# The order of the score groups within a head pair, in a windowed-attention and gated-MLP kernel

## The chip, the cores and the metric

The kernel runs on one core of a Trainium2 chip. The metric is the device time of one execution in microseconds (us); lower is better. A core has five engines with instruction streams of their own: PE (TensorE, matrix multiplications and transposes), ACT (ScalarE, exponentials, GELU and copies), DVE (VectorE, elementwise work), POOL (GpSimd) and SP (SyncE, which issues DMAs). Each engine takes its instructions in program order; between engines, semaphores hold an instruction back until what it needs is there.

## The reference, cut to what matters

Attention with a window of 128 positions and 4 sink positions, over a batch of 4, 8 heads, 768 positions and 64 values a head; then a gated MLP block over the 512 attention outputs of a position.

```python
scores = scale * np.matmul(q, k.transpose(0, 1, 3, 2))
keep = is_sink | in_window          # pos < 4, or 0 <= rel < 128
a = np.exp(np.where(keep, scores, -1e9) - max); a = a / a.sum(-1)
x = np.matmul(a, v)                 # heads side by side: 768 x 512 per batch
h = gelu(x @ w_in); u, v = halves of h
v_n = (v - mean) / sqrt(var + 1e-6) * g_ln
v_s = einsum('ts,bsd->btd', w_sg, v_n) + b_sg
out = x + (u * v_s) @ w_out
```

## The kernel before, in words

The work is cut into 16 head pairs, n = 0 to 15, four to a batch. The order of all instructions is written out by hand: the program order of the Python text is the order on each engine, and nothing reorders it. PSUM has these pools: `ps_s`, two buffers for scores; `ps_t`, one buffer for the transposes of k and q; `ps_a`, one for the attention outputs; `ps_m`, two for the MLP's products.

For each pair the main loop does the following.

- `repack` (L182): POOL casts k and q of pair n + 2 to bf16, and issues the load of v.
- `score(n, g)` (L223, L227), for g = 0, 1, 2: four matmuls on PE, two for each head, put the scores of 256 keys into one `ps_s` buffer. The two heads lie on rows 0 to 63 and 64 to 127, so these matmuls use 64 rows each (64*128 in the profile), where all others use 128. One exponential on ACT takes the scores from PSUM to the tile `ex`.
- `values(n - 1, i)` (L268, L271, L274), for i = 0 to 5: the pair before is multiplied with its v; i = 0 to 2 go behind score 0 and i = 3 to 5 behind score 1. After each three, DVE divides by the sums (L278, L279).
- `keys(n + 1)` (L188, L195): behind score 0's values, PE transposes k of the next pair into `ps_t`, and ACT copies that to `kT`. POOL copies the sink keys (L205) from it to a tile `sk`.
- `keep_band(n, g)` (L234): DVE multiplies the exponentials by the mask.
- `queries(n + 1)` (L188, L195): behind score 1's values and mask, PE transposes q of the next pair, and ACT copies that to `qT`. From pair 4 on this goes through `ps_t`, the buffer that the keys use; before, through `ps_m`.
- `spread`: puts in fillers, which are pieces of the batch before: `spatial_weights` (L171), then eight spatial groups (L346 on PE, L349 and L352 on DVE) and six projections (L357 on PE, L360 on DVE).
- `sinks(n)` (L238, L240): one matmul of 128 rows gives the scores of the sink positions for the later queries, in a `ps_s` buffer, and one exponential on ACT takes them to `exs`. It stands behind the fillers of g = 2.

After each pair whose number can be divided by 4 (from pair 4 on), the remaining fillers are put out and the hidden stage of the finished batch follows (`hidden`: L296, L298, L300 for one half of h, L308, L311 for the other), with the values of that pair in between. The pair behind it (5, 9, 13) therefore has no values of a pair before it, and its first exponential comes behind an ACT table load, since the hidden stage uses GELU. Pair 15 has no next pair, hence no `keys` and no `queries`.

Of the kernel before, what the change touches and what calls it, by code (L numbers as in the profile page):

```python
# [17 lines left out]
def kernel(  # L18
# [23 lines left out]
    HP = H // 2  # L42
# [31 lines left out]
    def load_qk(n):  # L74
        b, hp = divmod(n, HP)
        pair = []
        for src, name in ((k, "k_sb"), (q, "q_sb")):
            dst = loads.tile([128, 2, NT, 64], F32, name=name)
            nc.sync.dma_start(out=dst, in_=src[b, 2 * hp:2 * hp + 2].rearrange(
                "h (p t) d -> p h t d", t=NT))  # L80
            pair.append(dst)
        qk[n] = pair

    def load_v(n):
        b, hp = divmod(n, HP)
        nc.gpsimd.dma_start(  # L86
            out=v_bufs[n % NV][:, :, :, 0:64],
            in_=v[b, 2 * hp:2 * hp + 2].rearrange("h (t p) d -> p h t d", p=128))
# [61 lines left out]
    def load_weights(n):  # L150
        if n < 4:
            half = slice(DF, d_ff) if n < 2 else slice(0, DF)
            cs = slice(KD // 2 * (n % 2), KD // 2 * (n % 2 + 1))
            nc.gpsimd.dma_start(
                out=w_in_sb[:, cs, half],
                in_=moe_w_in.rearrange("(c p) f -> p c f", p=128)[:, cs, half])
        elif n == 4:
            for c in (slice(0, HT), slice(HT, NT)):
                nc.gpsimd.dma_start(
                    out=wsg_sb[:, c, :],  # L160
                    in_=moe_w_sg.rearrange("(c p) s -> p c s", p=128)[:, c, :])
        elif n == 5:
            nc.gpsimd.dma_start(out=b_bc, in_=moe_b_sg.partition_broadcast(128))
            nc.gpsimd.dma_start(out=g_sb, in_=moe_g_ln.rearrange("(c p) -> p c", p=128))
            nc.gpsimd.dma_start(out=w_out_sb,
                                in_=moe_w_out.rearrange("(c p) f -> p c f", p=128))
# [11 lines left out]
    def repack(n, eng):  # L178
        packed[n] = []
        for src, name in zip(qk.pop(n), ("k_bf", "q_bf")):  # L180
            flat = work.tile([128, NT, 128], BF16, name=name)
            eng.tensor_copy(flat.rearrange("p t (h d) -> p h t d", h=2), src)  # L182
            packed[n].append(flat)
# [15 lines left out]
    def keys(n):  # L199
        kT, sk = kT_bufs[n % NB], sk_bufs[n % NB]  # L200
        kps = to_columns(packed[n][0], ps_t, "tp")
        copy(nc.scalar, kT, kps)
        for hl in range(2):
            rows = slice(64 * hl, 64 * hl + 64)
            nc.gpsimd.tensor_copy(sk[rows, 32 * hl:32 * hl + n_sink], kT[rows, 0:n_sink])  # L205

    def queries(n, eng, pool, tag):
        qps = to_columns(packed.pop(n)[1], pool, tag)
        qTs[n] = work.tile([128, S], BF16, name="qT")
        copy(eng, qTs[n], qps)  # L210

    def score(n, g):
        kT, qT = kT_bufs[n % NB], qTs[n]
        if g == 0:
            exps[n] = work.tile([128, NT * 512 - 256], BF16, name="ex")
        ex = exps[n]
        sc = ps_s.tile([128, 2, 512], F32, name="sc", tag="s")
        w = 0
        for j in (2 * g, 2 * g + 1):
            n_q = min(256, S - 128 * j)  # L220
            for hl in range(2):
                rows = slice(64 * hl, 64 * hl + 64)
                nc.tensor.matmul(sc[:, hl, w:w + n_q], kT[rows, 128 * j:128 * (j + 1)],  # L223
                                 qT[rows, 128 * j:128 * j + n_q], start=True, stop=True)
            w += n_q
        part = ex[:, 1024 * g:1024 * g + 2 * w].rearrange("p (h c) -> p h c", h=2)
        nc.scalar.activation(out=part, in_=sc[:, :, 0:w], func=AF.Exp, scale=scale)  # L227

    def keep_band(n, g):
        w = 1024 if g < HT - 1 else 768  # L230
        part = exps[n][:, 1024 * g:1024 * g + w]
        m = mask0 if g == 0 else mask
        m = m.rearrange("p a c -> p (a c)") if g < HT - 1 else mask_end
        nc.vector.tensor_mul(part, part, m)  # L234

    def sinks(n):
        scs = ps_s.tile([128, 2, 512], F32, name="scs", tag="s")
        nc.tensor.matmul(scs[:, 0, 0:NS], sk_bufs[n % NB], qTs.pop(n)[:, 256:S],  # L238
                         start=True, stop=True)
        nc.scalar.activation(out=exs_bufs[n % NB][0:32 + n_sink],  # L240
                             in_=scs[0:32 + n_sink, 0, 0:NS], func=AF.Exp, scale=scale)

    def by_dma(n):
        return n >= HP and n % HP < HP - 1

    def columns(n):
        b, hp = divmod(n, HP)
        xps = to_columns(x_sb[b][:, hp], ps_m, "mm")
        nc.vector.tensor_copy(xT[b][:, hp, :], xps.rearrange("c t p -> c (t p)"))  # L249

    def values(n, i):
        b, hp = divmod(n, HP)
        if hp == 0 and i == 0:
            x_sb[b] = work.tile([128, HP, NT, 128], BF16, name="x")
            xT[b] = work.tile([128, HP, S], BF16, name="xT")
        ex, exs, v_sb = exps[n], exs_bufs[n % NB], v_bufs[n % NV]
        c, m = divmod(i, HT)
        if m == 0:
            avs[n] = ps_a.tile([128, HT, 2, 65], F32, name="av", tag="av")
        av = avs[n]  # L260

        def probs(j, hl, half):
            at = 1024 * (j // 2) + hl * min(512, S - 256 * (j // 2) + 128)
            at += 256 * (j % 2) + 128 * half
            return ex[:, at:at + 128]

        for hl in range(2):
            nc.tensor.matmul(av[:, m, hl, :], probs(i, hl, 0), v_sb[:, hl, i, :],  # L268
                             start=(m == 0 and hl == 0), stop=False)
            if i >= 1:  # L270
                nc.tensor.matmul(av[:, m, hl, :], probs(i - 1, hl, 1),  # L271
                                 v_sb[:, hl, i - 1, :], start=False, stop=False)
        if i >= 2:
            nc.tensor.matmul(av[:, m], exs[:, 128 * (i - 2):128 * (i - 1)],  # L274
                             vsink[:, n], start=False, stop=(m == HT - 1))
        if m == HT - 1:
            rcp = inverses[:, 2 * n + c]
            nc.vector.reciprocal(rcp, av[:, :, :, 64:65])  # L278
            nc.vector.tensor_mul(  # L279
                x_sb[b][:, hp, HT * c:HT * (c + 1), :].rearrange(  # L280
                    "p i (h d) -> p i h d", h=2),
                av[:, :, :, 0:64], rcp.to_broadcast([128, HT, 2, 64]))
        if i == NT - 1 and by_dma(n):
            nc.sync.dma_start_transpose(
                out=xT[b][:, hp, :].rearrange("p (i q) -> p i q", i=NT),
                in_=x_sb[b][:, hp].rearrange("p i d -> p (i d)"))
# [80 lines left out]
    def fill(count=1):  # L367
        for _ in range(count):
            if fillers:
                fillers.pop(0)()  # L370
# [147 lines left out]
    for n in range(NP):  # L518
        if n + 2 < NP:
            repack(n + 2, G)  # L520
            load_v(n + 2)
        load_weights(n)
        value = (lambda i: values(n - 1, i)) if n > 0 and valued < n - 1 else (lambda i: None)
        points = (HT + 1) * ((HP - n) % HP)

        def spread(left):
            fill(-(-len(fillers) // (points + left)))

        for g in range(HT):
            score(n, g)  # L530
            if g < 2:
                for i in range(HT * g, HT * (g + 1)):
                    value(i)
            if g == 0 and n + 1 < NP:
                keys(n + 1)
                if n < HP:
                    queries(n + 1, A, ps_m, "mm")
            keep_band(n, g)
            if g == 1 and n + 1 < NP and n >= HP:
                queries(n + 1, A, ps_t, "tp")  # L540
            spread(HT + 1 - g)
        if n + 3 < NP:
            load_qk(n + 3)
        sinks(n)
        if n > 0 and valued < n - 1 and not by_dma(n - 1):
            columns(n - 1)
        spread(1)
        valued = n - 1
        if n % HP == 0 and n > 0:
            fill(len(fillers))  # L550
            hidden(n // HP - 1, [lambda i=i: values(n, i) for i in range(NT)])
            valued = n
# [51 lines left out]
```

## Time and profile before

| | |
|---|---|
| median of 3 runs | 185.49 us (185.37 to 187.05) |
| profiled execution | 184.96 us, its span 183.1 us |
| PE busy | 156.4 us, 85% of the span |
| DVE busy | 150.6 us, 82% |
| ACT busy | 115.7 us, 63% |
| POOL busy | 58.3 us, 32% |
| pair 5 begins | 43.88 us after the span's start |
| pair 15's score 0 | 139.88 us |

The span runs from the first to the last instruction; the rest of the execution's time lies around it. A row of the profile names an engine, a line of the kernel, an operation, and what it writes and reads ("ex<-sc"). Behind a bar come the busy time in total, the mean duration of one in ns, and the idle time of the engine just before these instructions with what ended it. In a timeline a row gives the start, the duration, the engine and the line; a bracket at its end holds the idle time before it and what released it. PE's matmuls overlap each other: one of 384 columns lasts 0.33 us, and the next starts 0.16 us after it.

### The profile page before, as it was taken

What the parts mean: (1) busy time and instruction counts of PE and PEld (TensorE: products, weight loads), DVE (VectorE), ACT (ScalarE), POOL (GpSimd) and SP (SyncE); (2) the same over time, 40 slices, a digit from 0 to 9 for tenths busy, and PEclk for the clock granted to TensorE, in tenths of its full rate; (3) what the DMA queues carried; (4) which work ended last, traced back from release to release, by engine and by line L of the source; (5) the groups of instructions that cost most, each with busy time, mean ns of one, the idle gap of its engine ahead of it and who ended that gap; (6) DMA issues with size and microseconds to landing.
All of it is one profiled execution on the core that took longest, in us unless ns stands there. A gap on an engine that the chain in (4) does not pass through costs nothing.

```text
span 183.1 us, 3710 instructions
## 1 busy us (share of the span) xinstructions
PE 156.4 (85%) x1397; PEld 88.4 (48%) x1407; DVE 150.6 (82%) x362; ACT 115.7 (63%) x159; POOL 58.3 (32%) x98
## 2 busy tenths in 40 slices
PE   0679778799689999899799998998999979998950
PEld 0436555456456555455455544563564444544410
DVE  5676888699779998698899988699999977888850
ACT  2398999767828668666967778778875706630000
POOL 7569999930050161422051070650000000000000
PEclk9999999999789999999999999999999999999997
DMA  5999999999934769996248579976202551000081
GB/s 178 251 313 251 259 271 270 187 203 227 189 58 32 215 68 257 307 186 46 56 162 82 173 223 186 363 57 42 47 0 43 132 194 67 0 0 4 27 294 39
DMA packets 47289, 27.27 MB, mean 149 GB/s; under 512 B 33632, under 2 KB 44128, under 8 KB 47264
## 3 DMA queue, kind: packets, MB, share of 16 engines
q1 hardware_dynamic: 19360, 20.65, 37.7%
q0 software_dynamic: 27904, 6.31, 36.6%
q8 instruction: 13, 0.21, 0.5%
q14 instruction: 12, 0.10, 0.2%
HBM read 24.81 MB, written 6.29 MB: 170 GB/s over the span
## 4 chain that ended last, share of the span: by engine, by line
PE 58%; DVE 17%; ACT 13%; issue 4%; DMA 3%; SPq 1%; POOL 1%; DVEq 0%
PE vs L346 13%; PE o_ps L357 11%; ACT ex L227 6%; PE sc L223 6%; PE hv L296 6%; PE hu L308 6%; PE cps L188 5%; DVE st L300 4%; PE av L268 4%; DMA q_sb<-in_q_dram 3%; ACT kT L195 2%; DVE vn L336 2%; PE av L271 2%; PE wps L171 2%; PE av L274 2%
## 5 line engine op out<-in xcount | busy, mean ns | idle before, releaser
L227 ACT ACTIVATE ex<-sc 128x1024 bf16<-128x1024 f32 (+1 forms) x48 | 45.6, 958 | 17.6 <-PE sc L223 17.3
L346 PE MATMUL vs<-wsgT,vn 128*128 128x384 bf16 x192 | 36.4, 326 | 3.3 <-DVE vn L336 1.4
L346 PEld LDWEIGHTS <-vn 128*128 128x128 bf16 x192 | 17.8, 98 | 16.6 <-DVE vn L336 4.0
L234 DVE TENSOR_TENSOR ex<-ex,mask 128x1024 bf16<-128x1024 bf16 x32 | 22.7, 709 | 3.6 <-ACT ex L227 3.6
L296 PE MATMUL hv<-w_in_sb,xT 128*128 128x512 bf16 x93 | 22.7, 379 | 2.2 <-DVE xT L249 1.7
L182 POOL CAST k_bf<-k_sb 128x768 bf16<-128x768 f32 x15 | 12.7, 847 | 36.9 <-DMA k_sb<-in_k_dram 22.4
L357 PE MATMUL o_ps<-w_out_sb,gT 128*128 128x512 bf16 x89 | 23.4, 379 | 0.9 <-DVE o_sb L360 0.6
L308 PE MATMUL hu<-xT,w_in_sb 128*128 128x384 bf16 x128 | 23.6, 325 | 0.0
L298 ACT ACTIVATE v_all<-hv 128x512 f32<-128x512 f32 x24 | 14.3, 597 | 11.8 <-PE hv L296 11.5
L349 DVE SCALAR_TENSOR_TENSOR gv<-vs,g_sb,b_bc 128x384 bf16<-128x384 f32 x32 | 19.6, 613 | 1.2 <-PE vs L346 1.2
L300 DVE BATCH_NORM_STATS2 st<-v_all 128x6 f32<-128x512 f32 x24 | 16.4, 682 | 4.9 <-ACT v_all L298 4.8
L223 PE MATMUL sc<-qT,kT 64*128 64x256 bf16 x192 | 19.1, 282 | 1.3 <-DVE qT L197 1.0
L268 PE MATMUL av<-v_sb,ex 128*128 128x65 bf16 x192 | 19.0, 198 | 1.4 <-DVE x L279 1.4
L311 ACT ACTIVATE uT<-hu 128x384 bf16<-128x384 f32 x32 | 15.7, 490 | 7.1 <-PE hu L308 6.9
L268 PEld LDWEIGHTS <-ex 128*128 128x128 bf16 x192 | 14.8, 100 | 9.0 <-issue 2.5
L279 DVE TENSOR_TENSOR x<-av,inverses 128x384 bf16<-128x384 f32 x32 | 17.8, 557 | 1.1
L360 DVE TENSOR_TENSOR o_sb<-o_ps,x 128x512 f32<-128x512 f32 x24 | 16.5, 688 | 2.0 <-PE o_ps L357 1.7
L205 POOL COPY sk<-kT 64x4 bf16<-64x4 bf16 x32 | 6.6, 206 | 34.4 <-ACT kT L195 33.5
L271 PE MATMUL av<-v_sb,ex 128*128 128x65 bf16 x160 | 17.3, 197 | 0.0
L86 POOL DMA_DIRECT2D v_sb<-in_v_dram x16 | 16.6, 1036 | 0.0
L182 POOL CAST q_bf<-q_sb 128x768 bf16<-128x768 f32 x15 | 14.6, 972 | 5.0 <-PE hu L308 2.1
L308 PEld LDWEIGHTS <-w_in_sb 128*128 128x128 bf16 x128 | 12.1, 97 | 8.3 <-issue 1.2
(72 smaller groups left out, 231.3 us busy)
## 6 DMA issues: line engine op xcount, KB each, us to landing
k_sb<-in_k_dram SPq DMA_DIRECT2D x16, 384.0 KB, 5.4
q_sb<-in_q_dram SPq DMA_DIRECT2D x16, 384.0 KB, 6.2
out_dram<-o_sb SPq DMA_DIRECT2D x24, 256.0 KB, 3.5
v_sb<-in_v_dram POOLq DMA_DIRECT2D x16, 192.0 KB, 7.2
wsg_sb<-in_moe_w_sg_dram POOLq DMA_DIRECT2D x2, 576.0 KB, 9.9
w_in_sb<-in_moe_w_in_dram POOLq DMA_DIRECT2D x4, 256.0 KB, 9.2
w_out_sb<-in_moe_w_out_dram POOLq DMA_DIRECT2D x1, 512.0 KB, 11.2
b_bc<-in_moe_b_sg_dram POOLq DMA_DIRECT2D x1, 384.0 KB, 10.0
```

Source lines behind the costliest of these rows:

```text
L182: eng.tensor_copy(flat.rearrange("p t (h d) -> p h t d", h=2), src)
L223: nc.tensor.matmul(sc[:, hl, w:w + n_q], kT[rows, 128 * j:128 * (j + 1)], qT[rows, 128 * j:128 * j + n_q], start=True, stop=True)
L227: nc.scalar.activation(out=part, in_=sc[:, :, 0:w], func=AF.Exp, scale=scale)
L234: nc.vector.tensor_mul(part, part, m)
L268: nc.tensor.matmul(av[:, m, hl, :], probs(i, hl, 0), v_sb[:, hl, i, :], start=(m == 0 and hl == 0), stop=False)
L271: nc.tensor.matmul(av[:, m, hl, :], probs(i - 1, hl, 1), v_sb[:, hl, i - 1, :], start=False, stop=False)
L296: nc.tensor.matmul(h_ps, xT[b][:, c, 128 * j:128 * (j + 1)], w_in_sb[:, c, DF:], start=(c == 0), stop=(c == KD - 1))
L300: nc.vector.bn_stats(out=st, in_=v_alls[b][:, j, :])
L308: nc.tensor.matmul(h_ps[:, 0:NH], w_in_sb[:, c, 128 * f:128 * (f + 1)], xT[b][:, c, NH * n:NH * (n + 1)], start=(c == 0), stop=(c == KD - 1))
L346: nc.tensor.matmul(vs[:, 0:NH], vns[b][:, si, 128 * f:128 * (f + 1)], wsgT[:, si, cols], start=(si == 0), stop=(si == NT - 1))
L349: nc.vector.scalar_tensor_tensor(out=gv, in0=vs[:, 0:NH], scalar=g_sb[:, f:f + 1], in1=b_bc[:, cols], op0=ALU.mult, op1=ALU.add)
L357: nc.tensor.matmul(o_ps, gTs[b][:, c, 128 * t:128 * (t + 1)], w_out_sb[:, c, :], start=(c == 0), stop=(c == KU - 1))
```

## The change

From pair 5 on (`n > HP`, with HP = 4), `score(n, 0)` and `score(n, 1)` are both put out at g = 0, with their exponentials, ahead of the values, the keys' transposes and the fillers of that step. At g = 1 no score is put out; the values 3 to 5, the mask, the queries and the fillers keep their places. At g = 2 `score(n, 2)` is followed at once by `sinks(n)`, which before stood behind the mask, the fillers of that step and the issue of the next loads. Pairs 0 to 4 stay as they are, and so do all shapes, tiles and buffers.

```diff
+        def pending(g):
+            if n > HP:
+                if g == 0:
+                    score(n, 0)
+                    score(n, 1)
+                elif g == 2:
+                    score(n, 2)
+                    sinks(n)
+            else:
+                score(n, g)
+
         for g in range(HT):
-            score(n, g)
+            pending(g)
             if g < 2:
                 for i in range(HT * g, HT * (g + 1)):
                     value(i)
@@
             spread(HT + 1 - g)
         if n + 3 < NP:
             load_qk(n + 3)
-        sinks(n)
+        if n <= HP:
+            sinks(n)
         if n > 0 and valued < n - 1 and not by_dma(n - 1):
             columns(n - 1)
         spread(1)
```

## The prediction

> **What bounds the kernel now.** I read the page first, then the time by stage, then the engines' own timelines pair by pair from pair 5 on (pairs count from 0), since only pairs 5 to 15 change. From the page:
>
> ```profile
> PE 156.4 (85%) x1397; PEld 88.4 (48%) x1407; DVE 150.6 (82%) x362; ACT 115.7 (63%) x159; POOL 58.3 (32%) x98
> ...
> L195 ACT COPY kT<-cps 128x768 bf16<-128x768 bf16 x16 | 12.7, 794 | 4.0 <-PE cps L188 4.0
> ```
>
> PE and DVE are both near full, ACT is not; an average says no more. The view by stage says more (columns: stretch, its length, busy time of PE, PEld, DVE, ACT, POOL, granted clock, DMA):
>
> ```profile
> 44.66:48.07 3.41, 1.55 (x24) 1.14 (x22) 2.54 (x6) 3.40 (x4) 0.37 (x2) 1.00 1.10 119
> 48.07:51.49 3.42, 3.42 (x29) 2.69 (x29) 2.70 (x5) 1.86 (x3) 0.82 (x1) 0.50 0.83 250
> 126.58:129.99 3.41, 2.22 (x18) 1.13 (x17) 3.08 (x7) 3.40 (x5) 0.36 (x2) 1.00 0.29 58
> 94.58:101.51 6.93, 6.93 (x77) 4.12 (x77) 6.67 (x16) 4.88 (x6) 2.21 (x4) 1.00 0.61 59
> ```
>
> The last row is pair 10: PE is busy for all of its 6.93 us, DVE for 6.67. In this pair PE is the bound and nothing that it issues waits; a wait added to PE there is paid in full as soon as DVE's small slack is no obstacle. The first three rows come back below, for the clock. Now pair 10 on PE and on ACT:
>
> ```profile
> 94.58 0.39 PE L223 MATMUL sc<-qT,kT 64*128 64x256 bf16 x4
> ...
> 95.28 0.50 PE L188 MATMUL cps<-iden,k_bf 128*128 128x128 bf16 x6
> 95.62 1.14 PE L346 MATMUL vs<-wsgT,vn 128*128 128x384 bf16 x6
> 96.69 0.39 PE L223 MATMUL sc<-qT,kT 64*128 64x256 bf16 x4
> 97.01 0.20 PE L268 MATMUL av<-v_sb,ex 128*128 128x65 bf16 x1
> ...
> 97.56 0.50 PE L188 MATMUL cps<-iden,q_bf 128*128 128x128 bf16 x6
> ```
>
> ```profile
> 95.02 1.02 ACT L227 ACTIVATE ex<-sc 128x1024 bf16<-128x1024 f32 x1 [0.71 <-PE sc L223]
> 95.94 0.79 ACT L195 COPY kT<-cps 128x768 bf16<-128x768 bf16 x1
> 97.12 1.02 ACT L227 ACTIVATE ex<-sc 128x1024 bf16<-128x1024 f32 x1 [0.39 <-PE sc L223]
> 98.09 0.80 ACT L195 COPY qT<-cps 128x768 bf16<-128x768 bf16 x1
> ```
>
> The reader should see the order on ACT: first exponential, copy of kT, second exponential, copy of qT. The transposes of k and of q share the single buffer of ps_t, so PE's q transposes (97.56) can't start before ACT has emptied it into kT (95.94 + 0.79 = 96.73). Here that leaves 0.83 us of slack. Where the slack is gone, in the first pair after a batch's hidden stage, it is a wait already:
>
> ```profile
> 127.25 1.02 ACT L227 ACTIVATE ex<-sc 128x1024 bf16<-128x1024 f32 x1
> 128.17 0.79 ACT L195 COPY kT<-cps 128x768 bf16<-128x768 bf16 x1
> ...
> 129.01 0.49 PE L188 MATMUL cps<-iden,q_bf 128*128 128x128 bf16 x6 [0.28 <-ACT kT L195]
> ```
>
> ```profile
> 45.31 0.39 PE L223 MATMUL sc<-qT,kT 64*128 64x256 bf16 x4
> 47.55 0.49 PE L188 MATMUL cps<-iden,q_bf 128*128 128x128 bf16 x6 [1.85 <-ACT kT L195]
> ```
>
> **The change, part by part.** No instruction is added or removed; three moves are made.
>
> *Move 1, on PE: score 1 directly behind score 0.* Score groups use 64 rows, all else 128 (the 64*128 and 128*128 in the rows). In pair 10 six L346 start 0.1625 us apart from 95.62, so the next slot is 96.595; after them comes score 1, and the values start at 97.01. The group with both changes of row form costs 0.42 us. The two score groups that already stand together in pair 0 start 0.40 us apart at 0.19 us between matmul starts, against 0.12 here, which makes about 0.23 us at this speed. So each merged group gives back 0.19 us of PE, 2.1 us over 11 pairs if nothing else moved; bounds 0.15 to 0.22. The Trainium skill, "TensorEngine Tiling (Array Packing)", Key Properties, says that changing the tiling mode drains TensorE; that speaks for the change, and it gives no price, so the sum stays with the rows.
>
> *Move 2, on ACT: the second exponential goes ahead of the kT copy.* This follows from the same edit, since each score issues its exponential. ACT then runs exponential, exponential, kT copy. From exponential to the next instruction ACT takes 0.92 us (95.02 to 95.94); for an exponential behind an exponential, pair 0 has one place (two merged, the second a short one of 0.81):
>
> ```profile
> 10.95 1.73 ACT L227 ACTIVATE ex<-sc 128x1024 bf16<-128x1024 f32 x2
> ```
>
> 1.73 - 0.81 is 0.92 again. So the kT copy starts 0.92 us later, measured from the first exponential. With T the start of score 0, the first exponential starts at T + 0.44, the kT copy at T + 2.28, ends at T + 3.07, and the q transposes can go at T + 3.12 (0.05 from copy end to PE, as at 128.17 + 0.79 and 129.01). PE arrives there at T + 2.98 - 0.19 = T + 2.79 in pairs whose filler is a spatial group (6, 7, 10, 14), and at T + 2.68 where it is a shorter projection (8, 11, 12: 2.87 in the trace, from 68.01 to 70.88). So PE now waits 0.33 and 0.44 us where it waited for nothing. Net of the 0.19 gained: +0.15 us in each of four pairs and +0.25 in each of three. Behind the waiting transposes on PE stand the next filler, score 2, the sink scores and two fillers; DVE's product or projection sum, ACT's qT copy and the third exponential wait for those, so the next thing late is everything. The bounds: -0.19 if the wait were covered, +0.35 if the exponentials slip by another 0.1.
>
> In pairs 5, 9 and 13 an ACT table load stands ahead of the first exponential (it starts at T + 1.9) and PE already waits for kT. There PE's 0.19 only lengthens the wait, and the whole 0.92 us is paid: q transposes at 129.93 instead of 129.01. Bounds 0.85 (a little regained from idle PE) and 1.3 (pair 5, where part of the following work falls to the half clock below).
>
> Pair 15 has no next pair, hence no kT copy: PE gains 0.19, but DVE works there without a gap from 139.99 to 145.90, and its first reciprocal would now wait 0.08 us for values that start later; I take -0.1, bounds -0.2 to 0.
>
> *Move 3: the sink scores directly behind score 2, ahead of a filler.* They join no row form (128*128), so no change is saved. Cost taken: 0. The cover: their exponentials are first read in the next pair's values, over 3 us later, their PSUM buffer (score 1's) was emptied over 2 us before, and the filler that they push back by 0.22 us feeds a DVE that is still on the last mask (100.19 to 100.75, with the filler's product at 100.66). If that cover were gone it would cost up to 0.2 us in each of 11 pairs; bounds 0 to +1 us in all. Queues: POOL's two small copies behind kT move by 0.92 us and POOL idles for microseconds around them; no wait moves past SP's loads, whose buffers the casts free as before.
>
> *Sum on the path:* 3 x 0.92 + 4 x 0.15 + 3 x 0.25 - 0.1 = **+4.0 us**.
>
> **The clock.** The first stage row shows a stretch of 3.41 us with PE busy 1.55 us; the next 3.42 us ran at a granted clock of 0.50. The third row shows 2.22 us busy, and the rows after it stay at 1.00. So somewhere between 1.55 and 2.22 us of work the clock is lost, for one stretch. After the change, PE in pair 13 has only two lone L346 (0.33 each) between 126.83 and 129.93; a stretch laid over that has about 1.0 us of work, well under 1.55, while one whose edge falls in the middle has over 2. Pair 9 is alike. Where the edges fall I can't know from one execution: with about half of all positions hitting, one of the two pairs is likeliest. Half a clock for 3.41 us costs 1.7 us of PE work, less some 0.2 spent waiting anyway: **+1.5 us**; bounds 0 and 3.0 for none and both. The Trainium skill, "TensorE: Matmul & The Clock Gate", What's actually happening, says that the clock halves after at least one idle window of some 3.4 us. Read strictly, 1.7 us of unbroken idle would not do it and the time would be that of the rival without a half stage; but the 44.66 row had a break of 1.85 us only and lost the clock, so I go by the row.
>
> 184.96 us, the profiled execution's own time (span 183.1 and 1.9 around it), + 4.0 + 1.5 = 190.5. The median of the runs, 185.49, lies 0.5 above that execution, so **191.0**.
>
> **The rivals.**
> *No further half stage* (0.26): waits as computed, the edges fall kindly or the threshold is lower: 189.5. For it: 2.22 us of work was enough.
> *Two half stages* (0.18): pairs 9 and 13 both, 192.5. Against it: a loss in pair 9 shifts pair 13 by about half a stretch.
> *DVE takes up the waits* (0.07): if DVE, not PE, set the pace (6.67 of 6.93 us), the 0.15 and 0.25 us would vanish in its backlog and only 3 x 0.92 remain: 185.49 + 2.7 = 188.2. Against it: in pair 10 no PE instruction waits for DVE.
> *The saved form changes win* (0.06), not slower: if PE reached the q transposes after the kT copy, all 11 merged groups would keep 0.19 us: 185.49 - 2.1 = 183.4. It decides if the copy ends before T + 2.7, that is 0.4 us sooner than I compute, or if the second exponential stood behind the copy on ACT. Against it: the program order of ACT. Half of it caught would be no change.
>
> **How the numbers follow.** The forecast has 0.43. The range 188.6 to 193.0 reaches from the rival with DVE's backlog to both half stages, with the bounds on the sink move. Within 1% is about what a measurement of this kernel can tell from no change; faster by over 1% gets 0.04, within 1% 0.05, slower 0.91.
>
> **What would show it.** Right: on ACT two exponentials in a row from pair 5 on, then kT; the q transposes waiting for kT in ten pairs, with 0.15 to 0.3 us of idle PE in seven (the profile counts from a matmul's end, some 0.16 us after the next could have started) and over 1.4 us in three; PE's idle before kT in total some 7 us instead of 2.6; a second stretch at 0.50 clock. Wrong: no wait before the q transposes, DVE with no gaps, or score groups that don't start about 0.23 us apart.

## The result, and the profile after

The changed kernel is slower: 191.38 us, the median of 4 runs (190.5 to 193.08), against 185.61 us for the kernel before on the same chip. The ratio is 1.034, with a 95% interval of 1.029 to 1.040. The forecast was 191.0 us, in a range of 188.6 to 193.0. Here and below, a ratio leaves out runs that lie more than 1.5% above the fastest of their kernel, so it can differ a little from the ratio of the medians.

The profiled execution is the slowest of the four, 193.08 us with a span of 191.3. Some 2.3 us of its distance to the profile before lies ahead of the change: pair 5 begins at 46.18 us instead of 43.88, because POOL waits longer for the first loads of k and q. So the pairs are compared by their lengths.

The page again, with its row of the q transposes, and then what PE waited for there, before and after:

```profile
PE 155.7 (81%) x1392; PEld 90.5 (47%) x1407; DVE 149.9 (78%) x362; ACT 114.5 (60%) x159; POOL 60.0 (31%) x98
...
L188 PE MATMUL cps<-iden,q_bf 128*128 128x128 bf16 x96 | 9.5, 245 | 10.4 <-ACT kT L195 8.5
```

```profile
PE cps L188 <- ACT kT L195: 2.6, 3, 1.8
```

```profile
PE cps L188 <- ACT kT L195: 8.5, 10, 2.9
```

The busy times hardly changed, and the span did. PE's idle time ahead of the q transposes that ends with the copy to kT is 8.5 us, in ten waits of at most 2.9; before it was 2.6 us, in three. This line names the place of the cost. Its size needs the stages too, since PE also saves some 2 us and loses clock.

The stages: pairs 6, 9 and 13 before.

```profile
54.39:61.31 6.92, 6.92 (x77) 4.11 (x77) 6.66 (x16) 4.88 (x6) 0.43 (x2) 1.00 0.65 62
...
86.97:94.58 7.61, 6.42 (x50) 3.27 (x49) 6.92 (x16) 6.51 (x8) 1.20 (x3) 1.00 0.48 131
...
125.34:132.96 7.62, 6.43 (x51) 3.29 (x51) 7.08 (x16) 6.51 (x8) 0.36 (x2) 1.00 0.14 28
```

And after. First the stretch that ends where the second half-clock stretch begins, that stretch, and one that kept its clock; then whole pairs: 6, 9 and 13.

```profile
91.84:95.25 3.41, 1.39 (x8) 0.41 (x6) 2.71 (x6) 3.40 (x4) 0.00 (x0) 1.00 0.39 71
95.25:98.66 3.41, 3.15 (x16) 1.59 (x17) 1.24 (x3) 0.96 (x3) 1.97 (x4) 0.50 0.66 217
132.80:136.21 3.41, 1.79 (x14) 0.82 (x13) 2.50 (x6) 3.38 (x5) 0.00 (x0) 1.00 0.29 58
...
57.38:64.44 7.06, 6.71 (x76) 4.31 (x77) 6.76 (x16) 4.71 (x6) 0.54 (x2) 1.00 0.62 61
...
90.86:100.85 9.99, 7.57 (x50) 3.83 (x51) 6.89 (x15) 6.49 (x8) 3.41 (x5) 0.83 0.37 100
...
132.23:140.76 8.53, 6.14 (x49) 3.28 (x49) 6.49 (x15) 6.49 (x8) 0.81 (x2) 1.00 0.12 25
```

An ordinary pair takes 7.06 us instead of 6.92, and PE is no longer busy all through it. Pair 13 takes 8.53 instead of 7.62. Pair 9, in which the clock halves, takes 9.99 instead of 7.61. Pair 10 on ACT and PE:

```profile
101.28 1.94 ACT L227 ACTIVATE ex<-sc 128x1024 bf16<-128x1024 f32 x2 [1.36 <-PE sc L223]
103.11 0.81 ACT L195 COPY kT<-cps 128x768 bf16<-128x768 bf16 x1
104.49 0.80 ACT L195 COPY qT<-cps 128x768 bf16<-128x768 bf16 x1 [0.58 <-PE cps L188]
```

```profile
100.85 0.61 PE L223 MATMUL sc<-qT,kT 64*128 64x256 bf16 x8
101.77 0.50 PE L188 MATMUL cps<-iden,k_bf 128*128 128x128 bf16 x6
102.10 1.14 PE L346 MATMUL vs<-wsgT,vn 128*128 128x384 bf16 x6
103.96 0.49 PE L188 MATMUL cps<-iden,q_bf 128*128 128x128 bf16 x6 [0.18 <-ACT kT L195]
```

The two exponentials stand in a row (x2), the copy ends at 103.92, and the q transposes start at 103.96, 3.11 us after score 0. And pair 9:

```profile
92.76 1.94 ACT L227 ACTIVATE ex<-sc 128x1024 bf16<-128x1024 f32 x2
94.59 0.81 ACT L195 COPY kT<-cps 128x768 bf16<-128x768 bf16 x1
```

```profile
92.75 0.79 PE L346 MATMUL vs<-wsgT,vn 128*128 128x384 bf16 x2 [0.20 <-DVE vn L336]
95.44 0.80 PE L188 MATMUL cps<-iden,q_bf 128*128 128x128 bf16 x6 [1.90 <-ACT kT L195]
96.04 2.12 PE L346 MATMUL vs<-wsgT,vn 128*128 128x384 bf16 x6
```

PE stands idle for 1.90 us, and then six L346 take 2.12 us instead of 1.14: the work behind the wait runs at half speed. The lengths of the pairs, in us, before, after, and by forecast:

| pairs | before | after | difference | forecast |
|---|---|---|---|---|
| 5 | 10.51 | 11.20 | +0.69 | +0.92 |
| 6, 7, 10, 14, each | 6.92 (7: 6.70) | 7.06 (7: 6.84) | +0.14 | +0.15 |
| 8, with the hidden stage | 18.96 | 19.58 | +0.62 | +0.25 |
| 11; 12 with the hidden stage | 6.48; 17.35 | 6.73; 17.60 | +0.25 each | +0.25 each |
| 9 | 7.61 | 9.99 | +2.38 | +0.92, and 1.5 for the clock |
| 13 | 7.62 | 8.53 | +0.91 | +0.92 |

From pair 5 to pair 14 that is 5.6 us in all, and by forecast 4.1 for the order on ACT and 1.5 for the clock.

### The profile page after: what moved, and what is told of

Same layout as the page of the kernel before. It is cut to its first block, busy times and chain, and to the rows that moved or that the text cites. A ratio compares the mean times of both kernels' runs of the same rounds, so it can differ in the third digit from the quotient of the medians.

```text
span 191.3 us, 3715 instructions
## 1 busy us (share of the span) xinstructions
PE 155.7 (81%) x1392; PEld 90.5 (47%) x1407; DVE 149.9 (78%) x362; ACT 114.5 (60%) x159; POOL 60.0 (31%) x98
## 4 chain that ended last, share of the span: by engine, by line
PE 36%; DVE 24%; ACT 23%; issue 8%; DMA 4%; SPq 1%; POOL 0%; DVEq 0%; ACTq 0%
ACT ex L227 12%; PE vs L346 10%; PE o_ps L357 8%; DVE st L300 6%; ACT kT L195 5%; DMA q_sb<-in_q_dram 4%; PE cps L188 4%; PE sc L223 4%; DVE vn L336 3%; PE hv L296 3%; PE hu L308 3%; DVE o_sb L360 2%; DVE gv L349 2%; DVE ex L234 2%; DVE mv L301 2%
## 5 line engine op out<-in xcount | busy, mean ns | idle before, releaser
L227 ACT ACTIVATE ex<-sc 128x1024 bf16<-128x1024 f32 (+1 forms) x48 | 44.4, 956 | 21.6 <-PE sc L223 21.4
L346 PE MATMUL vs<-wsgT,vn 128*128 128x384 bf16 x192 | 36.5, 332 | 2.9 <-issue 0.8
L346 PEld LDWEIGHTS <-vn 128*128 128x128 bf16 x192 | 18.5, 99 | 14.9 <-DVE vn L336 2.6
L357 PE MATMUL o_ps<-w_out_sb,gT 128*128 128x512 bf16 x90 | 22.6, 378 | 1.4 <-DVE o_sb L360 1.0
L349 DVE SCALAR_TENSOR_TENSOR gv<-vs,g_sb,b_bc 128x384 bf16<-128x384 f32 x32 | 19.6, 614 | 4.3 <-PE vs L346 4.3
L205 POOL COPY sk<-kT 64x4 bf16<-64x4 bf16 x32 | 8.6, 269 | 43.8 <-ACT kT L195 42.8
L223 PE MATMUL sc<-qT,kT 64*128 64x256 bf16 x192 | 17.4, 283 | 1.2 <-DVE qT L197 1.0
L188 PE MATMUL cps<-iden,q_bf 128*128 128x128 bf16 x96 | 9.5, 245 | 10.4 <-ACT kT L195 8.5
L195 ACT COPY qT<-cps 128x768 bf16<-128x768 bf16 x15 | 12.0, 803 | 8.0 <-PE cps L188 8.0
```

The source lines that it names most:

```text
L195: eng.copy(dst, src)
L346: nc.tensor.matmul(vs[:, 0:NH], vns[b][:, si, 128 * f:128 * (f + 1)], wsgT[:, si, cols], start=(si == 0), stop=(si == NT - 1))
L349: nc.vector.scalar_tensor_tensor(out=gv, in0=vs[:, 0:NH], scalar=g_sb[:, f:f + 1], in1=b_bc[:, cols], op0=ALU.mult, op1=ALU.add)
L357: nc.tensor.matmul(o_ps, gTs[b][:, c, 128 * t:128 * (t + 1)], w_out_sb[:, c, :], start=(c == 0), stop=(c == KU - 1))
```

## The experiments

The theory: the loss is the second exponential ahead of the kT copy on ACT, by way of the single buffer that the k and q transposes share; where PE waits longest, it loses its clock as well. The rivals are the sink move, the later values, and a loss in proportion to the pairs changed.

**1. The copy first.** Scores 0 and 1 stay together on PE, and only the second exponential goes back behind the copy: `later=True` keeps it in a list `late`, and `late.pop()()` issues it.

```diff
-                    score(n, 1)
+                    score(n, 1, later=True)
...
             if g == 0 and n + 1 < NP:
                 keys(n + 1)
...
+            if late:
+                late.pop()()
             keep_band(n, g)
```

> The matmuls of scores 0 and 1 stay together on PE, but the second exponential is issued behind the kT copy, as it was before the change. Theory (the order on ACT makes the loss): the q transposes wait for kT only in the three pairs that did before, 2.6 us in all; no half-clock stretch is added; PE keeps its 0.19 us in pairs 6, 7, 8, 10, 11, 12 and 14, less what DVE's own 6.75 us a pair leaves of it: 184.2 to 184.8 us, 0.8 to 1.4 us under the kernel before. Rival (moving the scores together harms by itself, through the values that start later, or the sink move): it stays above 187. Rival (DVE sets the pace): 185.6, no change.

Measured: 184.05 us against 185.55, ratio 0.991 (0.987 to 0.995). That is 0.15 below the range that I gave, in which DVE's 6.75 us a pair was to take a part of the gain; it didn't. The values start later here too, so it isn't they that cost. The order on ACT makes the whole loss, and without it the moves give a gain. The second profile of this version, taken in experiment 9, shows pair 10:

```profile
95.34 1.02 ACT L231 ACTIVATE ex<-sc 128x1024 bf16<-128x1024 f32 x1 [1.31 <-PE sc L225]
96.41 0.80 ACT L195 COPY kT<-cps 128x768 bf16<-128x768 bf16 x1
97.11 1.03 ACT L231 ACTIVATE ex<-sc 128x1024 bf16<-128x1024 f32 x1
...
98.20 0.80 ACT L195 COPY qT<-cps 128x768 bf16<-128x768 bf16 x1
```

```profile
94.90 0.61 PE L225 MATMUL sc<-qT,kT 64*128 64x256 bf16 x8
...
97.67 0.50 PE L188 MATMUL cps<-iden,q_bf 128*128 128x128 bf16 x6
```

The q transposes start 2.77 us after score 0 with no wait before them; the copy ended 0.46 us earlier (96.41 + 0.80 = 97.21). The stage:

```profile
94.90:101.62 6.72, 6.72 (x77) 4.28 (x77) 6.51 (x16) 4.83 (x6) 2.17 (x4) 1.00 0.61 59
```

PE is busy all through, and pairs 6, 10 and 14 take 6.71 us, 0.21 less than before: the saved change of row form, in full.

**2. The sink move alone.**

```diff
-                if g == 0:
-                    score(n, 0)
-                    score(n, 1)
-                elif g == 2:
-                    score(n, 2)
+                score(n, g)
+                if g == 2:
                     sinks(n)
```

> Only the third move: the sink scores directly behind score 2 from pair 5 on, the score groups where they were before. Theory: no cost, 185.6 us within 0.4, pair 8 perhaps up to 0.2 later where a projection is pushed back behind the sink scores. Rival (the sink move carries part of the loss): 186.5 or more. Rival (it gains): under 185.

Measured: 185.11 against 185.55, ratio 0.999 (0.995 to 1.003). The median is 0.1 us below the range that I gave, and the interval of the ratio holds no change: the sink move costs nothing that can be measured. An ordinary pair takes 6.92 us as before. The profile of this run has no half-clock stretch before the tail, and pair 5 takes 9.41 us in it instead of 10.51.

**3. The merged scores alone,** with `sinks(n)` where it was for all pairs.

> Only scores 0 and 1 together with their exponentials, the sink scores where they were before. Theory: the whole loss, as the changed kernel, 190.5 to 192. Rival (the sink move carries part of it): 187 to 189.5.

Measured: 191.7 against 185.55, ratio 1.034 (1.028 to 1.040), the ratio of the whole change. In its profile one half-clock stretch lies in pair 5, which takes 11.62 us, and the other in pair 13, which takes 9.94; pair 9 takes 8.53.

**4. The pairs behind a hidden stage left out.**

```diff
-            if n > HP:
+            if n > HP and n % HP != 1:
...
-        if n <= HP:
+        if n <= HP or n % HP == 1:
             sinks(n)
```

> The change in all pairs from 6 on except 9 and 13, so that the pairs behind a hidden stage (5, 9, 13), whose first exponential stands behind a table load, keep the old order. Theory: 3 x 0.92 us and the added half-clock stretch are gone; four waits of a net 0.15 and three of 0.25 stay, with pair 15 about +1.3: 186.9 us, range 186.4 to 187.5, one half-clock stretch as before. Rival (the loss is spread evenly over the pairs): 8 of 11 pairs changed would leave 73 per cent of 5.8 us, 189.8. Rival (waits in the ordinary pairs vanish in DVE's backlog): 185.6.

Measured: 186.37 against 185.55, ratio 1.008 (1.003 to 1.012), or +0.6 to +2.2 us where 1.3 was worked out and a loss spread evenly would have given 4.2. In the profile pairs 9 and 13 take 7.62 us again, pairs 6, 10 and 14 keep 7.06, and pairs 6 to 14 together take 1.3 us more than before. Both parts of the loss are there as forecast: the small waits add up, and DVE doesn't take them up. One thing was not as expected: this execution, the fastest of its ten at 185.01 us, has no half-clock stretch in the pairs at all, and pair 5 takes 9.41 us.

**5. The waits filled.** The changed kernel, and PE works through the waits of pairs 5, 9 and 13.

```diff
+                if n % HP == 1:
+                    busy_work(16 if n == HP + 1 else 9)
                 queries(n + 1, A, ps_t, "tp")
```

> The changed kernel with idle PE time filled: ahead of the q transposes of pairs 5, 9 and 13, where PE waits 1.7 to 3 us for kT, PE runs 16, 9 and 9 matmuls of 390 columns (0.165 us each) whose result nothing uses. Theory (the half-clock stretches follow from idle PE): no stretch at 0.5 clock from pair 5 to 15, the waits for kT as long as before in sum of work and idle: 188.3 to 189.7, some 2 us under the changed kernel, though PE does 5.6 us of work more. Rival (the half clock has another cause): 190.5 to 193, stretches as before.

Measured: 188.85 against 185.13, ratio 1.017 (1.011 to 1.023). PE has over 5 us of work more than in the changed kernel, and the time is some 3 us less by the ratios (1.017 against 1.034). On this chip the changed kernel's median is 191.87 us (experiment 6), though one of its four runs took 188.03. The stages of pairs 9 and 13:

```profile
88.05:96.58 8.53, 7.64 (x58) 4.16 (x58) 7.07 (x15) 6.49 (x8) 2.52 (x4) 1.00 0.41 115
127.97:136.50 8.53, 7.64 (x58) 4.16 (x60) 6.53 (x15) 6.48 (x8) 0.80 (x2) 1.00 0.13 25
```

Both take 8.53 us at full clock, the 7.62 of before and 0.91 of waiting, and no stretch from pair 5 to 15 is at half clock. That isn't the luck of one execution: over whole runs the mean granted clock is 0.989 to 0.997 in these six, and 0.963 to 0.983 in the eight runs of the changed kernel. So idle PE is what loses the clock. What is left, 3.7 us, is the order on ACT by itself; the sum had 4.0. (Pair by pair at full clock, with the 9.41 of experiment 2 for pair 5, it is 3.8.)

**6. The changed kernel once more,** beside experiments 5, 7 and 8.

> The changed kernel once more, beside the three others on one chip: 190.5 to 192.5, and by theory a half-clock stretch in pair 5 and in one of pairs 9 and 13, not always the same one.

Measured: a median of 191.87 (188.03 to 192.65, 4 runs); the profile is of the 192.65. The stretches before and in its half clocks:

```profile
90.56:93.97 3.41, 1.18 (x9) 0.43 (x7) 2.49 (x6) 3.13 (x4) 0.21 (x1) 1.00 0.55 110
93.97:97.39 3.42, 3.08 (x17) 1.38 (x16) 1.39 (x3) 1.42 (x2) 2.45 (x5) 0.50 0.48 177
131.52:134.93 3.41, 1.51 (x10) 0.53 (x8) 3.05 (x8) 3.40 (x4) 0.00 (x0) 1.00 0.29 58
134.93:138.35 3.42, 3.10 (x16) 1.49 (x17) 1.25 (x3) 1.06 (x2) 0.81 (x2) 0.50 0.00 0
```

Here the clock halves in pairs 9 and 13 both (10.11 and 9.94 us) and not in pair 5 (10.03 us). The expectation of one in pair 5 and one in 9 or 13 was wrong for this execution: where the stretches fall differs from one execution to the next. The four times spread over 4.6 us, and the lowest lies 2.5 us under the expected range. That the stretches make this spread is likely, but only the profiled execution shows where its own lie.

**7. Another buffer for the q transposes,** the order on ACT left as changed.

```diff
-                queries(n + 1, A, ps_t, "tp")
+                queries(n + 1, A, ps_m, "mm")
```

> The changed kernel, ACT order and all, but from pair 5 on the q transposes go through ps_m (where the fillers' products lie) instead of the one ps_t buffer that they share with the k transposes. Theory (the loss is the wait for that one buffer, not the later copies as such): no wait of the q transposes for kT from pair 5 on, not even in pairs 5, 9 and 13; no half-clock stretch in 9 or 13; 183.5 to 185, at or under the kernel before. Rival (ACT's later copies delay something else too, or the fillers now lack a buffer): 187 or more.

Measured: 185.92 against 185.13, ratio 1.004 (1.000 to 1.008). PE's waits for kT are gone from pair 5 on, and most of the loss with them, so it was the wait for this one buffer. But the time missed its range, because the fillers' buffers are not free either. The waits of PE in pair 5:

```profile
PE cps L188 <- DVE wsgT L173: 2.5, 1, 2.5
```

The q transposes now wait until DVE has emptied a filler's product, and that copy stands behind the first mask, which waits for the first exponential behind the table load. In pair 9 it is the next filler that lacks a buffer (0.87 us, <-DVE gv L349). Pairs 9 and 13 take 7.84 us instead of 7.62, pairs 6, 10 and 14 the good 6.71. The profile is of a run of 187.84 us: behind the wait in pair 5 two half-clock stretches follow each other, and the pair takes 11.78 us.

**8. Both: the copy first and the other buffer.**

> Scores 0 and 1 together, the second exponential behind the kT copy, and the q transposes of pairs 6 to 15 through ps_m. Theory: the waits for kT of pairs 5, 9 and 13 go as well (2.0, 0.6 and 0.4 us in the kernel before, as far as the masks and score 2 behind them don't wait for ACT instead): 182.8 to 184.2, at or a little under the copy-first version's 184.05. Rival (the fillers lack the buffer): slower than the copy-first version.

Measured: 186.23 against 185.13, ratio 1.007 (1.003 to 1.011), slower than the copy-first version alone. The rival that I had named holds: the same 2.5 us of waiting for wsgT in pair 5, and 7.84 and 7.85 us in pairs 9 and 13. Beside the copy-first order, moving the wait to the pool of the fillers costs more than it saves.

**9. The copy first, with pair 5's wait filled,** and the copy-first version again beside it. The first has `busy_work(10)` ahead of pair 5's q transposes.

> The copy-first version with 10 matmuls of 390 columns, whose result nothing uses, ahead of the q transposes of pair 5, where PE waits 2 us for kT in the kernel before as well. Theory (idle PE loses the clock): no half-clock stretch from pair 5 to 15 in any position of the edges, so pair 5 takes 9.2 to 9.5 us always, against 9.4 to 10.5 with and without one before: 183.0 to 183.8 us. Rival (no effect of idle PE): as copy-first, 184.05, or later by the added work.

> The copy-first version once more beside it: 184.05 us within 0.5, or 0.7 to 1.1 per cent under the kernel before; pairs 6, 10 and 14 at 6.71 us.

Measured: 183.79 us for the filled one, ratio 0.992 (0.989 to 0.995); 184.06 for the copy-first version, ratio 0.993 (0.990 to 0.997); before 185.19. In the profile the filled one has no half clock in the pairs, and pair 5 takes 9.41 us, where copy-first took 10.05 with a half-clock stretch. Its twelve runs have a mean granted clock of 0.989 to 0.997, those of copy-first 0.970 to 0.995. The mechanism is there, but the medians differ by 0.3 us only and the intervals overlap, so a gain from filling is not shown. Both versions beat both kernels, the one before by 0.7 to 0.8%.

## Why the prediction was right, point by point

*PE is the bound in ordinary pairs.* Right: the small waits were paid in full (experiment 4), and the saved 0.19 us came back in full as 0.21 once the waits were gone (experiment 1). The rival with DVE's backlog is out.

*Score groups 0.23 us apart.* Right, with some luck. In the trace after, score 1 starts 0.23 us after score 0 in every pair from 5 on, and the 8 matmuls leave the row form once. The working has a slip: 0.40 us times 0.12/0.19 makes 0.25 us, not 0.23, and the saving by it 0.17 us, where 0.21 was measured.

*The copy ends 0.92 us later, the q transposes go at T + 3.12.* Right: 3.11 or 3.12 in every ordinary pair. The net +0.15, +0.25 and +0.92 were measured as +0.14, +0.25 and +0.91, in the pairs without another disturbance. PE's idle time for kT ahead of the q transposes, named as some 7 us, came to 8.5. In pairs 9 and 13 score 1 now runs ahead of PE's wait for vn (0.6 and 0.8 us before, 0.2 and none after), and that time turns up in the wait for kT instead.

*Pair 5.* The term was too large, and outside its bounds of 0.85 to 1.3. I took the 0.92 us of the kT copy whole. Without a half-clock stretch on either side it is +0.62 (10.03 in experiment 6 against 9.41 in experiment 2); with one on both sides it depends on where the stretch falls, +0.69 in the profile after and +1.11 in that of experiment 3. The q transposes do start 0.91 us later (4.58 us after score 0 instead of 3.67), but 0.3 us come back behind them. Experiment 2, then experiment 6:

```profile
47.98 0.49 PE L188 MATMUL cps<-iden,q_bf 128*128 128x128 bf16 x6 [1.84 <-ACT kT L195]
48.48 0.96 PE L171 MATMUL wps<-iden,wsg_sb 128*128 128x128 bf16 x12
49.38 0.34 PE L223 MATMUL sc<-qT,kT 64*128 64x256 bf16 x4
```

```profile
50.62 0.49 PE L188 MATMUL cps<-iden,q_bf 128*128 128x128 bf16 x6 [2.87 <-ACT kT L195]
50.96 0.83 PE L171 MATMUL wps<-iden,wsg_sb 128*128 128x128 bf16 x12
51.72 0.34 PE L223 MATMUL sc<-qT,kT 64*128 64x256 bf16 x4
```

From the q transposes to score 2 it is 1.40 us in the first and 1.10 in the second. In the first, the fillers (L171) start while DVE still copies the two products before them out of `ps_m` (L173, 47.88 to 48.90); in the second these copies (49.61 to 50.63) are over. So a part of the longer wait for kT took the place of a wait for these buffers, as far as the times tell.

*Pair 8.* The term was +0.25, and the profile after shows +0.62. The other 0.37 us is one mask on DVE that took 0.94 us instead of 0.56, while POOL cast the next pair's k at the same time:

```profile
76.91 0.94 DVE L234 TENSOR_TENSOR ex<-ex,mask_end 128x768 bf16<-128x768 bf16 x1 [0.43 <-ACT ex L227]
```

```profile
76.61 0.82 POOL L182 CAST k_bf<-k_sb 128x768 bf16<-128x768 f32 x1 [6.44 <-DMA k_sb<-in_k_dram]
```

In experiment 6 the cast begins at 76.22, behind the mask (75.59 to 76.15), the mask takes 0.56 us, and pair 8 takes 19.20, +0.24. So this belongs to the execution, by when the load lands, and not to the change. No run tries it by itself, but the twelve profiles hold 192 masks of this size. The 145 that meet no cast of POOL took 0.54 to 0.57 us, and so did the 16 in whose course a cast begins. Of the 31 that begin behind the start of a cast, 26 took 0.63 to 1.17 us and ended some 0.41 us after it; the other five, of 0.56 to 0.57 us, found less than 0.2 us of it left or, in one case, began 4 ns behind its start. So a mask that finds a cast under way is held up by it.

*Pair 15.* I took -0.1. From its start to the end the profiles of the kernels with merged scores give 43.07 to 43.45 us, against 43.25 before: too small to tell.

*The sink move at nothing.* Right (experiment 2).

*The clock, +1.5.* Right in size: a half-clock stretch cost 9.99 - 8.53 = 1.46 us in pair 9, and 1.41 in pair 13 of experiment 3. That it is one stretch was a guess about the edges; in pairs 9 and 13 the profiles show one, one and two. The rule that I weighed against the row, from the Trainium skill's page "TensorE: Matmul & The Clock Gate" (What's actually happening), asks for an idle window of some 3.4 us. The trace after lost the clock behind a stretch with 1.39 us of work and a longest break of 1.90 us, which ends 0.19 us behind that stretch. Here the measurement decides for the row.

*The sum.* That it came within 0.4 us of the median is in part luck: pair 5 lies 0.23 us under its term and pair 8, by an accident of the execution, 0.37 over, and with none or two half-clock stretches in pairs 9 and 13 the time would have been 1.5 us off either way.

*The rival that gains.* I gave its order on ACT as the condition ("if the second exponential stood behind the copy") and 183.4 us as its price. With that condition met, experiment 1 has 184.05: the gain is 0.21 us in each of the seven ordinary pairs, 1.5 us. It is not 0.19 in all eleven, since in pairs 5, 9 and 13 PE still waits for kT, and of pair 15 too little can be told.

## What to carry to other kernels

When two pieces of work are put together for one engine, list what each of them issues on the other engines, and look which short instruction there now stands behind a long one. Here 0.2 us saved on PE put 0.92 us ahead of a copy that empties a single buffer; putting the copy back in front turned a loss of 3% into a gain of 0.8%. In the ordinary pairs the wait on the saturated engine was paid in full, and where it was long it was in part paid again in clock.

## What the runs showed of the hardware

In the profiles of all these kernels, between pair 5 and the tail, the granted clock fell from full to half behind each stretch of 3.41 us that held 0.54 to 1.55 us of PE's busy time, and behind none that held 1.57 (experiment 6, in pair 5) or more. That is a little under half of the stretch, and no whole idle stretch is needed. The stretches lie on one grid in an execution: the two half clocks of experiment 6 start 40.96 us apart, 12 times 3.413. The stretch with 1.57 us and the one behind it:

```profile
46.19:49.61 3.42, 1.57 (x26) 1.23 (x23) 2.50 (x7) 3.39 (x4) 0.00 (x0) 1.00 1.55 162
```

```profile
49.61:53.02 3.41, 2.24 (x34) 1.94 (x35) 2.71 (x7) 2.68 (x5) 0.81 (x2) 1.00 0.86 52
```

Between them lies PE's wait of 2.87 us, cut in two by the edge at 49.61, and the clock stayed. In pair 13 of the same execution two breaks of 0.58 and 1.52 us left 1.51 us of work in a stretch, and the clock fell. So the busy time within a stretch tells it, not the length of a break.

A half clock lasted one stretch, with 2.88 us or more of PE's busy time in it. The one exception is pair 5 of experiment 7, where the first of two held 2.64 us:

```profile
49.88:53.29 3.41, 2.64 (x22) 1.98 (x23) 2.46 (x6) 1.68 (x3) 0.81 (x2) 0.50 0.83 76
53.29:56.70 3.41, 2.94 (x19) 2.11 (x19) 1.72 (x4) 1.28 (x2) 1.76 (x3) 0.50 0.53 184
```

The edges of the stretches lie elsewhere in each execution, so the same kernel has the half clock in one place or another, at 1.1 to 1.6 us each in the kernel before, the changed one and that of experiment 3, and 0.64 in pair 5 of the copy-first version (10.05 against the filled 9.41). Work without a use in the wait kept the clock (experiments 5 and 9).
